# Attention into two mixture stages on one core: row maxima from a bf16 view of the f32r keys, one maximum row in the scores, v's scale through PSUM

## The chip, the cores and the metric

One core of a Trainium2 chip. The metric is the device time of one execution in microseconds (us). Engines are named as in the profile: PE is TensorE (PEld its weight loads), DVE VectorE, ACT ScalarE, POOL GpSimd, SP the engine whose queue issues the DMAs.

## The reference, cut to what matters

```python
# q, k, v: (2, 8, 1152, 64)
q_pool = q.reshape(B, H, S // 2, 2, D).mean(axis=3)          # 576 queries a head
scores = scale * np.matmul(q_pool, k.transpose(0, 1, 3, 2))
scores = scores - np.max(scores, axis=-1, keepdims=True)
attn = np.exp(scores)
attn = attn / (np.sum(attn, axis=-1, keepdims=True) + 1e-09)
attn_out = np.matmul(attn, v)
# then on x = attn_out as (1152, 512):
p = domain_probs / (domain_probs.sum(-1, keepdims=True) + 1e-09)
out = sum(p[:, e:e+1] * (np.maximum(x @ w1[e], 0.0) @ w2[e]) for e in range(4))
# then (out @ m1) * (out @ m2) @ m3 @ m_out
```

The maximum is only a shift of the exponent: the same shift stands in the numerator and in the sum.

## The kernel before

The 16 heads go through as eight pairs. Of a pair i, head s (0 or 1) has nine blocks of 128 keys. `plan_scores` makes scores with keys on partitions: for each block, two bf16 matmuls of `K2`, `Q2` (low parts, and in the first rows the maximum and a constant against rows of -1) and two f32r matmuls of `K1`, `Q1`, into a PSUM tile `s`. ACT takes the exponential into `pf` (line 581), POOL makes its low part `pl` (line 592), and `plan_av` multiplies both by the two halves of v (`vt`, lines 614 and 616).

While pair i's scores and products run, pair i+1 is made ready, all on the same engines:

- `plan_k`: PE transposes the keys into PSUM (`kt`, line 278, first two thirds, then the last third). ACT copies them as f32r words (`KAB`, line 281) and once more as bf16 (`KB`, line 284). DVE takes the remainder `KL` (line 287).
- `plan_v`: DVE takes v's absolute row maxima (`vm`, line 493), PE spreads them over the partitions (`vp`, line 497), and `bounds` on DVE (lines 481, 484, 485) makes the scale `vs` in three steps: mask the exponent, multiply and bound, invert. The second step reads and writes SBUF.
- `plan_q`: PE transposes the pooled queries (`qt`, line 345), ACT copies them as f32r (`QH`, line 357), then twice as bf16 into `QZ` (lines 354, 358), where each head's queries stand on their own 64 rows and the other rows are zero. DVE takes the remainder `QL` (line 348). POOL copies a last piece (line 352).
- `plan_max`: PE multiplies `QZ` by `KB` into PSUM tiles `mp` (line 415, three matmuls of 384 columns a query block), DVE reduces each (line 418). When a head's blocks are done, PE transposes the maxima (`mr`, line 452), ACT rounds them to bf16 (`mh`, line 456), DVE takes what that left (`ml`, line 460), and SP writes the two as rows 0 and 1 of `Q2` with four DMAs (lines 465, 466). Row 2 holds a constant shift.
- `plan_spread`: SP copies `KAB`, `KL`, `QH`, `QL`, `QZ` to `K1`, `K2`, `Q1`, `Q2`.

The first pair has short ways of its own: `plan_k_now`, and `turn_now`, which transposes the maxima split into two bf16 parts (`MT`, lines 439 to 441).

The order on each engine is written out by hand. Every step is put into an agenda with a time (18 units a pair), the agenda is sorted, and each engine gets its instructions in that order. The constants at the head of the file (`VR`, `VE`, `TURNS`, `KT`, ...) are those times.

Two PSUM work tiles serve all the preparing: `w0` (two banks) and `w1` (one bank), one buffer each. In `w0` come `kt`'s first part, `qt` and the wide `mp` in turn; in `w1` `mr`, `kt`'s last part, `vp` and the narrow `mp`. So a PE instruction that writes one of them waits until the readers of the tile before are done, and what stands behind it on PE waits too.

After the attention come four experts (`up`, `dn`) and the second mixture (`wf`, `gt`, `o`), from 257 us of the span on.

Of the kernel before, what the change touches and what calls it, by code (L numbers as in the profile page):

```python
# [11 lines left out]
TURNS = (1.13, 1.53, 1.73, 3.03)  # L12
TURN0 = (0.05, 0.45, 0.55, 0.65)
KH = 0.39
# [9 lines left out]
KS = 0.1  # L24
KS0 = 0.01
# [11 lines left out]
VE = 1.85  # L37
# [82 lines left out]
def tile_kernel(ctx: ExitStack, tc: tile.TileContext, q, k, v, dp, w1, w2, mw1, mw2, mw3, mwo, out):  # L120
# [79 lines left out]
    MT = k_p.tile([P, 2, NB + 1], F32, name="MT")  # L200
# [6 lines left out]
    KAB, KL, KB, QH, QL = {}, {}, {}, {}, {}  # L207
# [52 lines left out]
    def plan_k(i, t):  # L260

        def start():
            KAB[i] = kq_p.tile([P, S], F32R, tag="kab", name=f"kab{i}")
            KB[i] = kq_p.tile([P, S], BF16, tag="kb", bufs=1, name=f"kb{i}")
            KL[i] = ha_p.tile([P, S], BF16, tag=f"ha{i % 2}", name=f"kl{i}")
# [3 lines left out]
        for g in range(2):  # L269
# [13 lines left out]
            def short(g=g, rows=rows):  # L283
                nc.scalar.copy(out=rows(KB[i]), in_=st[g][:, :, :PC])

# [7 lines left out]
            at(t + KT[g] + KH + KS, short)  # L293
            at(t + KT[g] + KH + KL_, lo)

    def plan_k_now(t):
# [3 lines left out]
        def pe(n):  # L300
            if n == 0:
                pft[0, 0] = ph_p.tile([P, NC, T], F32, tag="pf", name="pf0_0")
                KAB[0] = kq_p.tile([P, S], F32R, tag="kab", name="kab0")
                KB[0] = kq_p.tile([P, S], BF16, tag="kb", bufs=1, name="kb0")
# [5 lines left out]

        def short(n):
            dst = KB[0][:, n * PC : (n + 1) * PC]
            if n == 1:
                nc.vector.tensor_copy(dst, st[n])
            else:
                nc.scalar.copy(out=dst, in_=st[n])
# [14 lines left out]
        for n in range(3):  # L331
            at(t + 0.1 * n, pe, n)
            at(t + 0.1 * n + KS0, short, n)
# [3 lines left out]
    def plan_q(i, t, tv):  # L337
# [12 lines left out]
        def one(lo, hi, to):  # L350
            if lo:
                nc.gpsimd.tensor_copy(QZ[64:128, to : to + hi - lo], f32(QH[i][64:128, lo:hi]))
            else:
                nc.scalar.copy(out=QZ[64:128, to : to + hi - lo], in_=st[0][64:128, lo:hi])
# [3 lines left out]
        at(tv + 0.02, lambda: nc.scalar.copy(out=QZ[0:64, :T], in_=st[0][0:64, :T]))  # L358
# [34 lines left out]
    def plan_max(i, s, times):  # L393
# [11 lines left out]
        def pe(j, g):  # L405
# [6 lines left out]
            for n, third in enumerate(THIRDS[g]):  # L412
                sl = slice(third * PC, (third + 1) * PC)
                o = j * P + (T + TL if s else 0)
                mm(ps[:, n, :PC], QZ[:, o : o + P], KB[i][:, sl], start=True, stop=True)  # L415
# [13 lines left out]
        def end():  # L429
# [7 lines left out]
            if (i, s) == (0, 0):  # L437
                mb = tiny.tile([P, NB + 1], BF16, tag="mb", bufs=1, name="mb")
                nc.vector.tensor_copy(mb, mf)
                nc.vector.tensor_copy(MT[:, 0, :], mb)  # L440
                nc.vector.tensor_tensor(out=MT[:, 1, :], in0=mf, in1=MT[:, 0, :], op=ALU.subtract)

        def turn_now():

            ps = work(0, "mr0").rearrange("p n c -> p (n c)")
            for j in range(NB + 1):
                nc.tensor.transpose(ps[0:2, j * P : (j + 1) * P], MT[:, :, j], ident)
            nc.scalar.copy(out=Q2[s][0:2], in_=ps[0:2, :T])
# [5 lines left out]
        def cut_hi():  # L454
            m = st["h"] = tiny.tile([NB + 1, P], BF16, tag="mh", bufs=1, name=f"mh{i}_{s}")
            nc.scalar.copy(out=m, in_=st["r"][: NB + 1, 0, :P])

        def cut_lo():
# [920 lines left out]
```

## Time and profile before

| what | value |
|---|---|
| median of 3 runs | 812.67 us (812.42 to 814.46) |
| span of the profiled execution | 809.9 us, of which the page gives no other time |
| busy PE, DVE, ACT, POOL | 779.1, 597.3, 404.1, 295.9 us |
| granted TensorE clock, mean | 0.999 |

The span runs from the first to the last instruction; the runs' times also hold what lies around it (812.67 against 809.9). A busy PE counts an instruction from its start to its modelled end, and matmuls overlap, so PE's share is no measure of how full it is; how far two matmuls start apart is.

### The profile page before, as it was taken

The numbers are of one execution on the slowest core, as the hardware profiler recorded it, in microseconds if no ns is written. First come the engines' busy times: TensorE is split into PE (matmuls) and PEld (weight loads), VectorE is DVE, ScalarE is ACT, GpSimd is POOL, SyncE is SP. The second block draws the span as 40 slices with busy tenths as digits, with TensorE's granted clock in tenths as the row PEclk, the third lists the DMA queues.
The fourth block names the chain that finished last, engine by engine and source line by source line (L and its number), as shares of the span: only waits on it lengthen the run. The fifth ranks groups of instructions, "written<-read, shape, count | busy, mean of one in ns | idle before, by whom it ended". The sixth has DMA issues, their size and how long they took to land.

```text
span 809.9 us, 15666 instructions
## 1 busy us (share of the span) xinstructions
PE 779.1 (96%) x6301; PEld 493.2 (61%) x6301; DVE 597.3 (74%) x1067; ACT 404.1 (50%) x738; POOL 295.9 (37%) x277
## 2 busy tenths in 40 slices
PE   7799999999999999999999999999999999999998
PEld 6477777777776555555555555555554446655787
DVE  6888888887966666779878999979878877872000
ACT  3665666566584443444434567545554545553111
POOL 5679877987760000001101125303331223442100
PEclk9999999999999999999999999999999999999999
DMA  7856765673610221223312333221476752200011
GB/s 173 210 134 144 170 142 121 161 176 74 153 54 2 70 90 51 79 79 105 104 63 94 104 105 101 82 78 53 121 140 121 175 128 71 93 1 1 18 49 52
DMA packets 87255, 79.70 MB, mean 98 GB/s; under 512 B 51024, under 2 KB 69712, under 8 KB 87184
## 3 DMA queue, kind: packets, MB, share of 16 engines
q1 hardware_dynamic: 87184, 78.72, 37.3%
q8 instruction: 49, 0.80, 0.4%
q14 instruction: 22, 0.18, 0.1%
HBM read 51.92 MB, written 2.36 MB: 67 GB/s over the span
## 4 chain that ended last, share of the span: by engine, by line
PE 74%; DVE 16%; DMA 4%; ACT 3%; issue 1%; SPq 1%; POOL 0%; ACTq 0%; DVEq 0%; POOLq 0%
PE dn L785 19%; PE up L745 18%; PE gt L1317 12%; PE o L1333 6%; PE wf L1286 5%; DVE mx L418 5%; PE av L616 4%; PE s L571 3%; PE mp L415 3%; DMA rw<-in_moe_w 2%; DVE vt L550 2%; PE av L614 2%; DMA rk<-in_k 1%; DVE w L716 1%; DMA Q<-qh 1%
## 5 line engine op out<-in xcount | busy, mean ns | idle before, releaser
L785 PE MATMUL dn<-w,h 128*128 128x512 f16 x840 | 184.2, 379 | 0.4 <-DVE h L756 0.4
L592 POOL TENSOR_TENSOR pl<-pf 128x576 f16<-128x576 f32 x141 | 163.9, 1190 | 16.2 <-ACT pf L581 15.6
L745 PEld LDWEIGHTS <-w 128*128 128x128 f16 x1152 | 111.5, 98 | 76.4 <-DVE w L716 1.0
L785 PEld LDWEIGHTS <-h 128*128 128x128 f16 x840 | 81.6, 98 | 97.2 <-issue 1.7
L581 ACT ACTIVATE pf<-s 128x576 f32<-128x576 f32 x144 | 91.6, 652 | 53.0 <-PE s L571 52.3
L745 PE MATMUL up<-xB,w 128*128 128x320 f16 x768 | 109.9, 299 | 0.5 <-DVE xB L834 0.5
L418 DVE TENSOR_REDUCE mx<-mp 128x1 f32<-128x768 f32 (+1 forms) x144 | 102.0, 751 | 10.6 <-PE mp L415 8.4
L884 POOL TENSOR_TENSOR wo<-wo,cv_a 128x512 f32<-128x512 f32 x20 | 25.8, 1293 | 224.9 <-DVE wo L881 126.9
L751 ACT ACTIVATE up<-up 128x320 f32<-128x320 f32 (+1 forms) x96 | 45.8, 477 | 114.7 <-PE up L745 105.0
L571 PE MATMUL s<-Q,K 128*128 128x288 bf16 (+1 forms) x576 | 97.0, 313 | 0.5 <-ACT pf L581 0.3
L745 PE MATMUL up<-xA,w 128*128 128x512 f16 x384 | 89.0, 379 | 0.3 <-DVE w L716 0.3
L616 PE MATMUL av<-vt,pf 128*128 128x65 f16 x720 | 83.7, 193 | 1.1 <-DVE XT L631 1.1
L616 PE MATMUL av<-vt,pl 128*128 128x65 f16 x720 | 84.4, 195 | 0.0
L756 DVE TENSOR_TENSOR h<-up,h 128x320 f16<-128x320 f32 (+1 forms) x94 | 50.1, 550 | 44.3 <-ACT h L752 43.9
L614 PE MATMUL av<-vt,pf 128*128 128x64 f16 x720 | 82.8, 193 | 0.0
L1317 PEld LDWEIGHTS <-mw 128*128 128x128 f16 x576 | 55.9, 98 | 36.9
L616 PEld LDWEIGHTS <-pf 128*128 128x128 bf16 x720 | 67.3, 99 | 9.0 <-DVE XT L631 2.1
L616 PEld LDWEIGHTS <-pl 128*128 128x128 f16 x720 | 66.9, 97 | 8.9 <-issue 3.9
L614 PEld LDWEIGHTS <-pf 128*128 128x128 bf16 x720 | 67.3, 98 | 4.8 <-issue 1.6
L415 PE MATMUL mp<-kb,QZ 128*128 128x384 bf16 x216 | 51.5, 325 | 14.3 <-DVE ql L348 6.2
L799 DVE SCALAR_TENSOR_TENSOR x2B<-dn,sh,x2B 128x512 f32<-128x512 f32 x75 | 52.9, 744 | 4.6 <-PE dn L785 3.9
L1317 PE MATMUL gt<-x2Bt,mw 128*128 128x320 f16 x384 | 53.5, 299 | 0.0
(189 smaller groups left out, 1182.0 us busy)
## 6 DMA issues: line engine op xcount, KB each, us to landing
rw<-in_moe_w SPq DMA_DIRECT2D x64, 512.0 KB
K<-kab SPq DMA_DIRECT2D x32, 288.0 KB
rk<-in_k SPq DMA_DIRECT2D x16, 288.0 KB
rv<-in_v SPq DMA_DIRECT2D x8, 576.0 KB
rq<-in_q SPq DMA_DIRECT2D x8, 512.0 KB
rw<-in_moe_w_out SPq DMA_DIRECT2D x8, 512.0 KB
Q<-qh SPq DMA_DIRECT2D x16, 144.0 KB
Q<-ql SPq DMA_DIRECT2D x16, 144.0 KB
```

The lines of the kernel that those rows point to most:

```text
L415: mm(ps[:, n, :PC], QZ[:, o : o + P], KB[i][:, sl], start=True, stop=True)
L418: nc.vector.tensor_reduce(out=mx[i, s][:, j, g : g + 1], in_=st.pop((j, g))[:, :, :PC], axis=AX.XY, op=ALU.max)
L571: mm(ps[:, n, :HALF], a[s][:, cs], b[s][:, n * HALF : (n + 1) * HALF], start=first, stop=not first,)
L581: nc.scalar.activation(out=two(pft[i, s][:, c, :]), in_=st["s"][:, :, :HALF], func=AF.Exp, scale=SCORE)
L592: nc.gpsimd.tensor_tensor(out=o, in0=f, in1=h, op=ALU.subtract)
L614: mm(t[:, j, 0:D], p, vt[s][:, c, 0:D], start=False, stop=False)
L616: mm(t[:, j, :], p, vt[s][:, c, D:], start=(c == 0 and n == 0), stop=(c == NC - 1 and n == 2))
L745: mm(p, w[:, a, c, fc * P : (fc + 1) * P], x[b][:, c, lo - o : hi - o], start=(c == 0 and a == b), stop=(c == KD - 1 and a == 1),)
L756: nc.vector.tensor_tensor(out=hl[:, fc, lo:hi], in0=st["p"], in1=hh[:, fc, lo:hi], op=ALU.subtract)
L785: mm(p, hid[n][a][:, fc, t * P : (t + 1) * P], w[:, b, fc, :], start=(fc == 0 and a == b), stop=(fc == 1 and a == 1),)
L799: nc.vector.scalar_tensor_tensor(out=acc, in0=st["p"], scalar=share, in1=acc, op0=ALU.mult, op1=ALU.add)
L1317: mm(p, mws[n][:, a, m * KD + c], x[:, b * KD + c, lo - o : hi - o], start=(c == 0 and a == b), stop=(c == KD - 1 and a == 1),)
```

## The change

Seven edits:

1. `KB` is gone. The matmuls for the maxima read the upper 16 bits of each f32r word of `KAB` as bf16, every second bf16 element of the row. The bf16 copies (ACT lines 284 and 316, DVE line 314) are gone.
2. `ml` and its two DMAs a head are gone: the maximum is one bf16 row of `Q2`, the constant is row 1.
3. `MT` and its three DVE steps are gone: the first pair's maxima are transposed as they are.
4. `mh` has two buffers where it had one.
5. In v's scale the masked exponents go to two columns of the PSUM tile `vp`, and the second step reads them there.
6. `vp` stands 0.95 units earlier in the agenda (`VE` 1.85 to 0.9).
7. ACT's two copies into `QZ` read `QH` in SBUF, where they read `qt` in PSUM.

```diff
--- before.py
+++ after.py
@@ -9,8 +9,8 @@
 from concourse.masks import make_identity
 
 TURN = 1.03
-TURNS = (1.13, 1.53, 1.73, 3.03)
-TURN0 = (0.05, 0.45, 0.55, 0.65)
+TURNS = (1.13, 1.53, 3.03)
+TURN0 = (0.05, 0.45, 0.65)
 KH = 0.39
 KL_ = 0.22
 QH_ = 1.05
@@ -21,8 +21,6 @@
 LO_DVE = ((), ())
 LASTD = ((3,), (1, 6))
 LOL = 2.45
-KS = 0.1
-KS0 = 0.01
 EX = 0.84
 EX2 = 0.85
 LO = 3.95
@@ -34,7 +32,7 @@
 VL = 1.96
 VL0 = -1.66
 VR = 4.22
-VE = 1.85
+VE = 0.9
 V1 = (5.5, 1.4)
 VL1 = 7.8
 QZ0 = 0.25
@@ -197,14 +195,14 @@
 
 
     QZ = k_p.tile([P, 2 * T], BF16, name="QZ")
-    MT = k_p.tile([P, 2, NB + 1], F32, name="MT")
     QP = k_p.tile([P, NB + 1, 2, D], F32, name="QP")
 
     PAIRS = [(i // (H // 2), 2 * (i % (H // 2))) for i in range(NPAIR)]
 
 
     rq, rt, rk, rv = {}, {}, {}, {}
-    KAB, KL, KB, QH, QL = {}, {}, {}, {}, {}
+    KAB, KL, QH, QL = {}, {}, {}, {}
+    upper = lambda ap: ap.bitcast(BF16).rearrange("p (c w) -> p c w", w=2)[:, :, 1]
     pft, pht, plt = {}, {}, {}
 
     def load_k(i):
@@ -261,7 +259,6 @@
 
         def start():
             KAB[i] = kq_p.tile([P, S], F32R, tag="kab", name=f"kab{i}")
-            KB[i] = kq_p.tile([P, S], BF16, tag="kb", bufs=1, name=f"kb{i}")
             KL[i] = ha_p.tile([P, S], BF16, tag=f"ha{i % 2}", name=f"kl{i}")
 
         at(t + KT[0], start)
@@ -280,9 +277,6 @@
             def hi(g=g, rows=rows):
                 nc.scalar.copy(out=rows(KAB[i]), in_=st[g][:, :, :PC])
 
-            def short(g=g, rows=rows):
-                nc.scalar.copy(out=rows(KB[i]), in_=st[g][:, :, :PC])
-
             def lo(g=g, rows=rows):
                 nc.vector.tensor_tensor(
                     out=rows(KL[i]), in0=st[g][:, :, :PC], in1=f32(rows(KAB[i])), op=ALU.subtract
@@ -290,7 +284,6 @@
 
             at(t + KT[g] + NEAR, pe)
             at(t + KT[g] + KH, hi)
-            at(t + KT[g] + KH + KS, short)
             at(t + KT[g] + KH + KL_, lo)
 
     def plan_k_now(t):
@@ -301,19 +294,11 @@
             if n == 0:
                 pft[0, 0] = ph_p.tile([P, NC, T], F32, tag="pf", name="pf0_0")
                 KAB[0] = kq_p.tile([P, S], F32R, tag="kab", name="kab0")
-                KB[0] = kq_p.tile([P, S], BF16, tag="kb", bufs=1, name="kb0")
                 KL[0] = ha_p.tile([P, S], BF16, tag="ha0", name="kl0")
             ps = work(1, "kt0_2") if n == 2 else ps_s.tile([P, 2, 512], F32, tag="s", name=f"kt0_{n}")
             st[n] = ps[:, 0, :PC]
             for m in range(3):
                 nc.tensor.transpose(st[n][:, m * P : (m + 1) * P], rk[0][:, 3 * n + m], ident)
-
-        def short(n):
-            dst = KB[0][:, n * PC : (n + 1) * PC]
-            if n == 1:
-                nc.vector.tensor_copy(dst, st[n])
-            else:
-                nc.scalar.copy(out=dst, in_=st[n])
 
         def hi(n):
             dst = KAB[0][:, n * PC : (n + 1) * PC]
@@ -330,7 +315,6 @@
 
         for n in range(3):
             at(t + 0.1 * n, pe, n)
-            at(t + 0.1 * n + KS0, short, n)
             at(t + 0.1 * n + 0.05, hi, n)
             at(t + 0.6 - 0.1 * n, lo, n)
 
@@ -351,11 +335,11 @@
             if lo:
                 nc.gpsimd.tensor_copy(QZ[64:128, to : to + hi - lo], f32(QH[i][64:128, lo:hi]))
             else:
-                nc.scalar.copy(out=QZ[64:128, to : to + hi - lo], in_=st[0][64:128, lo:hi])
+                nc.scalar.copy(out=QZ[64:128, to : to + hi - lo], in_=f32(QH[i][64:128, lo:hi]))
 
         at(t, pe)
         at(tv, lambda: nc.scalar.copy(out=QH[i], in_=st[0][:, :T]))
-        at(tv + 0.02, lambda: nc.scalar.copy(out=QZ[0:64, :T], in_=st[0][0:64, :T]))
+        at(tv + 0.02, lambda: nc.scalar.copy(out=QZ[0:64, :T], in_=f32(QH[i][0:64])))
         at(tv + QL_, lo)
         tz = tv + (QZ0 if i == 1 else QZ1)
         at(tz, one, 0, NB * P, T + TL)
@@ -412,7 +396,7 @@
             for n, third in enumerate(THIRDS[g]):
                 sl = slice(third * PC, (third + 1) * PC)
                 o = j * P + (T + TL if s else 0)
-                mm(ps[:, n, :PC], QZ[:, o : o + P], KB[i][:, sl], start=True, stop=True)
+                mm(ps[:, n, :PC], QZ[:, o : o + P], upper(KAB[i])[:, sl], start=True, stop=True)
 
         def reduce(j, g):
             nc.vector.tensor_reduce(
@@ -434,36 +418,26 @@
                 nc.vector.reduce_max(mf[:, :NB], mx[i, 1][:, :NB], axis=AX.X)
                 nc.vector.reduce_max(mf[:, NB:], mx[i, 0][:, NB], axis=AX.X)
             st["f"] = mf
-            if (i, s) == (0, 0):
-                mb = tiny.tile([P, NB + 1], BF16, tag="mb", bufs=1, name="mb")
-                nc.vector.tensor_copy(mb, mf)
-                nc.vector.tensor_copy(MT[:, 0, :], mb)
-                nc.vector.tensor_tensor(out=MT[:, 1, :], in0=mf, in1=MT[:, 0, :], op=ALU.subtract)
 
         def turn_now():
 
             ps = work(0, "mr0").rearrange("p n c -> p (n c)")
             for j in range(NB + 1):
-                nc.tensor.transpose(ps[0:2, j * P : (j + 1) * P], MT[:, :, j], ident)
-            nc.scalar.copy(out=Q2[s][0:2], in_=ps[0:2, :T])
+                nc.tensor.transpose(ps[0:1, j * P : (j + 1) * P], st["f"][:, j : j + 1], ident)
+            nc.scalar.copy(out=Q2[s][0:1], in_=ps[0:1, :T])
 
         def turn():
             ps = st["r"] = work(1, f"mr{i}_{s}")
             nc.tensor.transpose(ps[: NB + 1, 0, :P], st["f"], ident)
 
-        def cut_hi():
-            m = st["h"] = tiny.tile([NB + 1, P], BF16, tag="mh", bufs=1, name=f"mh{i}_{s}")
+        def cut():
+            m = st["h"] = tiny.tile([NB + 1, P], BF16, tag="mh", name=f"mh{i}_{s}")
             nc.scalar.copy(out=m, in_=st["r"][: NB + 1, 0, :P])
 
-        def cut_lo():
-            m = st["l"] = tiny.tile([NB + 1, P], BF16, tag="ml", bufs=1, name=f"ml{i}_{s}")
-            nc.vector.tensor_tensor(out=m, in0=st["r"][: NB + 1, 0, :P], in1=st["h"], op=ALU.subtract)
-
         def place():
-            for n, m in enumerate((st["h"], st["l"])):
-                dst = Q2[s][n : n + 1]
-                nc.sync.dma_start(out=dst[:, : NB * P], in_=m[:NB])
-                nc.sync.dma_start(out=dst[:, NB * P :], in_=m[NB : NB + 1, r])
+            dst = Q2[s][0:1]
+            nc.sync.dma_start(out=dst[:, : NB * P], in_=st["h"][:NB])
+            nc.sync.dma_start(out=dst[:, NB * P :], in_=st["h"][NB : NB + 1, r])
 
         e = times[-1] + 1 + ME
         at(e, end)
@@ -471,17 +445,18 @@
             at(e + TURN, turn_now)
             at(e + TURN + 0.01, warm, WARM_T)
             return
-        for d, f in zip(TURNS if i else TURN0, (turn, cut_hi, cut_lo, place)):
+        for d, f in zip(TURNS if i else TURN0, (turn, cut, place)):
             at(e + d, f)
 
 
     vs = {}
 
-    def bounds(p, up, down, low, top=2.0**-14):
+    def bounds(p, up, down, low, top=2.0**-14, mid=None):
+        mid = up if mid is None else mid
         nc.vector.tensor_scalar(
-            out=up.bitcast(I32), in0=p.bitcast(I32), scalar1=0x7F800000, scalar2=None, op0=ALU.bitwise_and
+            out=mid.bitcast(I32), in0=p.bitcast(I32), scalar1=0x7F800000, scalar2=None, op0=ALU.bitwise_and
         )
-        nc.vector.tensor_scalar(out=up, in0=up, scalar1=top, scalar2=low, op0=ALU.mult, op1=ALU.max)
+        nc.vector.tensor_scalar(out=up, in0=mid, scalar1=top, scalar2=low, op0=ALU.mult, op1=ALU.max)
         nc.vector.reciprocal(out=down, in_=up)
 
     def plan_v(i, t, te):
@@ -498,7 +473,7 @@
 
         def keep():
             x = vs[i] = tiny.tile([P, 2], F32, tag="vs", bufs=3, name=f"vs{i}")
-            bounds(st["p"][:, 0, :2], x, x, 2.0**-100)
+            bounds(st["p"][:, 0, :2], x, x, 2.0**-100, mid=st["p"][:, 0, 2:4])
 
         at(t, rows)
         at(te, spread)
@@ -893,8 +868,8 @@
         for s in range(2):
             nc.gpsimd.memset(Q2[s][0:64], 0.0)
             nc.gpsimd.memset(K2[s][0:64], 0.0)
-            nc.gpsimd.memset(K2[s][0:3], -1.0)
-            nc.gpsimd.memset(Q2[s][0:3], -SHIFT)
+            nc.gpsimd.memset(K2[s][0:2], -1.0)
+            nc.gpsimd.memset(Q2[s][0:2], -SHIFT)
             nc.gpsimd.memset(vt[s][:, :, 128:129], 1.0)
         nc.vector.memset(idle, 0.0)
         nc.vector.memset(QP[TL:P, NB], 0.0)
```

DVE, the place where pair 3 is made ready during pair 2 (`vt` is v's low part, `kl` the keys' remainder, `ql` the queries' remainder). Before, it reads:

```order
L550 SCALAR_TENSOR_TENSOR vt_119<-rv_752,vs_1073,vt_119 128x9x64
L460 TENSOR_TENSOR ml_1_1511<-mr_1_1490,mh_1_1504 5x128
L287 TENSOR_TENSOR kl_1494<-kt_0_1495,kab_1492 128x768
L493 TENSOR_REDUCE vm<-rv_1340 128x2
L287 TENSOR_TENSOR kl_1494<-kt_1_1528,kab_1492 128x384
L481 TENSOR_SCALAR vs_1641<-vp_1633 128x2
L484 TENSOR_SCALAR vs_1641<-vs_1641 128x2
L485 RECIPROCAL vs_1641<-vs_1641 128x2
L348 TENSOR_TENSOR ql_1582<-qt_1583,qh_1581 128x576
```

Now the same stretch reads:

```order
L525 SCALAR_TENSOR_TENSOR vt_119<-rv_736,vs_1008,vt_119 128x9x64
L281 TENSOR_TENSOR kl_1462<-kt_0_1463,kab_1461 128x768
L468 TENSOR_REDUCE vm<-rv_1311 128x2
L281 TENSOR_TENSOR kl_1462<-kt_1_1493,kab_1461 128x384
L456 TENSOR_SCALAR vp_1560<-vp_1560 128x2
L459 TENSOR_SCALAR vs_1566<-vp_1560 128x2
L460 RECIPROCAL vs_1566<-vs_1566 128x2
L332 TENSOR_TENSOR ql_1544<-qt_1545,qh_1543 128x576
```

`ml` is gone, and the middle step of the scale reads `vp`. The scale stood ahead of `ql` already; only for pair 1 it stands behind it, before and now.

ACT, the same place (`pf` are the exponentials of pair 2's scores). Before, it reads:

```order
L456 CAST mh_1_1504<-mr_1_1490 5x128
L281 CAST kab_1492<-kt_0_1495 128x768
L284 CAST kb_1493<-kt_0_1495 128x768
L581 ACTIVATE pf_0_1425<-s_0_3_1483 128x576
L281 CAST kab_1492<-kt_1_1528 128x384
L284 CAST kb_1493<-kt_1_1528 128x384
L581 ACTIVATE pf_0_1425<-s_0_4_1532 128x576
L581 ACTIVATE pf_0_1425<-s_0_5_1570 128x576
L357 CAST qh_1581<-qt_1583 128x576
L354 CAST QZ<-qt_1583 64x512
L358 CAST QZ<-qt_1583 64x576
```

Now the same stretch reads:

```order
L435 CAST mh_1_1472<-mr_1_1459 5x128
L278 CAST kab_1461<-kt_0_1463 128x768
L556 ACTIVATE pf_0_1394<-s_0_3_1452 128x576
L278 CAST kab_1461<-kt_1_1493 128x384
L556 ACTIVATE pf_0_1394<-s_0_4_1497 128x576
L556 ACTIVATE pf_0_1394<-s_0_5_1534 128x576
L341 CAST qh_1543<-qt_1545 128x576
L338 CAST QZ<-qh_1543 64x512
L342 CAST QZ<-qh_1543 64x576
```

Two copies are gone, and `QZ` comes from `qh`.

PE, the same place, around `vp` (`av` are the products with v). Before, it reads:

```order
L616 MATMUL av_1_1459<-vt_120,pl_1_1160 128x65
L497 LDWEIGHTS ones
L497 MATMUL vp_1633<-vm,ones 128x2
L616 LDWEIGHTS pf_1_1159
L616 MATMUL av_1_1459<-vt_120,pf_1_1159 128x65
L571 LDWEIGHTS K_0_123
```

Now the same stretch reads:

```order
L591 LDWEIGHTS pl_1_1133
L591 MATMUL av_1_1428<-vt_120,pl_1_1133 128x65
L472 LDWEIGHTS ones
L472 MATMUL vp_1560<-vm,ones 128x2
L591 LDWEIGHTS pf_1_1132
L591 MATMUL av_1_1428<-vt_120,pf_1_1132 128x65
```

`vp` stood just ahead of a block of scores, 33 products with v behind `qt`; now 9 of them stand between `qt` and `vp`, and the 24 others stand behind it. Nothing else moves on PE.

## Rows read from the trace of the kernel before

**Rows 1.** Windows: start:end, length, busy us of PE, PEld, DVE, ACT, POOL, clock, DMA.

```profile
79.00:106.00 27.00, 25.14 (x387) 20.53 (x386) 22.85 (x39) 16.90 (x30) 23.02 (x22) 1.00 0.63 148
```

**Rows 2.** Waits, 24 to 215 us: who waited for whom, total us, times, longest.

```profile
PE mp L415 <- DVE ql L348: 6.2, 6, 1.3
...
PE mp L415 <- DVE mx L418: 5.1, 9, 1.0
...
PEld kt L278 <- DVE ml L460: 3.9, 7, 1.5
```

**Rows 3.** Timeline of PE, 81 to 90 us: start, duration, [idle before <-releaser].

```profile
86.56 0.17 PE L497 MATMUL vp<-vm,ones 128*128 128x2 bf16 x1
...
87.38 0.67 PE L571 MATMUL s<-Q,K 128*128 128x288 bf16 x4
89.01 0.65 PE L415 MATMUL mp<-kb,QZ 128*128 128x384 bf16 x3 [0.96 <-DVE ql L348]
```

**Rows 4.** Chain of waits, 79 to 107 us: start, time on the chain, what.

```profile
101.14 0.51 PE s L571 x4
...
101.72 0.49 PE mp L415 x3
102.21 0.06 PE av L616 x2
```

**Rows 5.** Timeline of DVE, 78 to 107 us.

```profile
82.22 0.27 DVE L460 TENSOR_TENSOR ml<-mr,mh 5x128 bf16<-5x128 f32 x1
83.41 0.96 DVE L287 TENSOR_TENSOR kl<-kt,kab 128x768 bf16<-128x768 f32 x1 [0.92 <-ACT kb L284]
...
85.55 0.55 DVE L287 TENSOR_TENSOR kl<-kt,kab 128x384 bf16<-128x384 f32 x1
...
86.99 1.00 DVE L484 TENSOR_SCALAR vs<-vs 128x2 f32<-128x2 f32 x1
...
88.11 0.75 DVE L348 TENSOR_TENSOR ql<-qt,qh 128x576 fp32r<-128x576 f32 x1
```

**Rows 6.** Timeline of POOL, 85.9 to 87.9 us.

```profile
86.82 1.15 POOL L592 TENSOR_TENSOR pl<-pf 128x576 f16<-128x576 f32 x1
```

**Rows 7.** Instructions that touch `vs`: duration ns min/median/max, first and last start.

```profile
L546 ACT ACTIVATE vt<-rv,vs x16: 771/781/785, 20.7 to 229.2; 128x576 f16<-128x576 f32 x16
L550 DVE SCALAR_TENSOR_TENSOR vt<-rv,vs,vt x16: 808/1684/2918, 35.2 to 232.4; 128x576 f16<-128x576 f32 x16
...
L481 DVE TENSOR_SCALAR vs<-vp x8: 149/159/160, 19.2 to 195.6; 128x2 int32<-128x2 int32 x8
L484 DVE TENSOR_SCALAR vs<-vs x8: 169/1014/1042, 19.4 to 195.8; 128x2 f32<-128x2 f32 x8
```

**Rows 8.** Timeline of ACT, 78 to 107 us.

```profile
81.88 0.80 ACT L281 CAST kab<-kt 128x768 fp32r<-128x768 f32 x1 [0.40 <-PE kt L278]
...
85.75 0.64 ACT L357 CAST qh<-qt 128x576 fp32r<-128x576 f32 x1
...
87.02 0.63 ACT L358 CAST QZ<-qt 64x576 bf16<-64x576 f32 x1
```

**Rows 9.** Waits, 0 to 34 us.

```profile
PEld kt L278 <- DVE ml L460: 0.9, 1, 0.9
```

**Rows 10.** Chain of waits, 0 to 36 us.

```profile
8.48 0.48 ACT kb L316
...
28.07 0.70 ACT kb L284
...
31.87 0.77 DVE ql L348
```

**Rows 11.** Timeline of PE, 0 to 36 us: the first pair's maxima.

```profile
17.87 0.70 PE L447 MATMUL mr<-ident,MT 128*2 128x128 f32 x5 [0.72 <-DVE MT L441]
```

**Rows 12.** Timeline of SP's queue, 78 to 107 us: the last DMA of `ml`.

```profile
103.50 0.52 SPq L466 DMA_DIRECT2D Q<-ml  x1
```

**Rows 13.** Timeline of PE, 104.9 to 105.5 us.

```profile
105.00 0.77 PE L571 MATMUL s<-Q,K 128*128 128x288 bf16 x4
```

## The prediction

> **What bounds the kernel now.** I read the windows first. In the 27 us in which one pair runs and the next is made ready, PE shows 25.14 us busy, DVE 22.85, POOL 23.02, ACT 16.90, at clock 1.00 [rows 1]. Busy PE is near the span, but its matmuls overlap, so the place to look is where PE starts nothing. After the attention the page's slices show PE at 9 tenths almost to the end, and the change touches nothing there: a gain in the attention shifts the rest, and that is all.
>
> The waits give the places [rows 2]. Once in six of the seven preparations PE stands before the maxima's first matmul (`mp`) until DVE has made `ql`; before the last transposes of the keys (`kt`) until DVE has made `ml`, 3.9 us in seven; and before a later `mp` until DVE has reduced, 5.1 us in nine. PE's timeline shows the first of these: four score matmuls start at 87.38, take 0.51 [rows 3, 4], and the next matmul starts at 89.01, so PE loses 1.12 us (the trace's own 0.96 counts from a modelled end).
>
> DVE's timeline shows why `ql` is late: the middle step of v's scale, two numbers a partition, takes 1.00 us from 86.99 to 87.99 [rows 5]. POOL's instruction beside it runs from 86.82 to 87.97 [rows 6]: the step ends 0.02 us behind it. Of eight such steps the median is 1.014 and the shortest 0.169; the step ahead of it, which reads PSUM and does as much, never takes over 0.160 [rows 7]. So the step waits for POOL's instruction, and an operand in PSUM is what sets the two apart.
>
> **The change part by part.** All times are on the clock of the profiled execution (span 809.9); the runs' median 812.67 lies 2.8 above it, and I take the same saving from the median.
>
> *The place of the wait for `ql`.* The first key copy ends at 82.68 [rows 8]; with `kb` gone `kl` starts then and not at 83.41 [rows 5], 0.73 sooner. Its second part ends at 86.10 - 0.73 = 85.37. PE reaches `vp` sooner too: 24 products with v stand behind it now, at 0.03 each [rows 4] 0.72, and the `kt` wait ahead is gone, about 0.3. That is 86.56 - 1.02 = 85.54 [rows 3], so `vp` goes without a wait, by 0.17. The scale's steps start 0.43 behind `vp`, less the first step that is 0.2 earlier still; at 0.16 each for the two that touch PSUM and as much for the third they end near 86.3. `qh` ends at 86.39 - 0.3 = 86.1 [rows 8], and `ql` runs from 86.3 to 87.05. The second `QZ` copy, which ended at 87.65 [rows 8], ends 0.3 sooner but reads SBUF: between nothing and 0.14 more each (ACT's 576 columns out of SBUF take 0.781 [rows 7], out of PSUM 0.63 to 0.64 [rows 8]); I take 0.1 each, as the copy does not scale, and get 87.55. PE arrives at 87.89 - 0.3 = 87.6. So `ql` is no longer the last, `QZ` and PE come out level, and I leave 0.1 as a wait: 6 x (1.12 - 0.1) = **6.1 us**.
>
> *The wait for `ml`.* The tile that `kt`'s last part needs comes free with ACT's `mh` and no more with DVE's `ml`, which stands behind the long `vt` step. Of 3.9 us [rows 2] the first preparation's 0.9 [rows 9] belongs to the next term, 3.0 is left. In the second preparation `vt` is at its longest, 2.918 [rows 7]; there PE, freed, meets `vp` before `kl` is done, and I give 0.5 back: **2.5 us**.
>
> *The first preparation.* `kb` (0.70) and `ql` (0.77) both lie on the chain [rows 10]. `kb` is gone, and `ql` runs beside the `QZ` copies, which no longer share its PSUM tile. 1.47, less 0.1 for SBUF: **1.4 us**.
>
> *The start.* PE waits 0.72 us for `MT` [rows 11]; transposing the maxima as they are ends that. A key copy of 0.48 leaves the chain at 8.48 [rows 10], as `kab` takes its place. The reductions behind it are paced by DVE, so not all of it arrives: between 0.7 and 1.2 in all, **1.0 us**.
>
> *The DMAs.* Thirty issues of some 0.5 us [rows 12] leave SP's queue. The last of `ml` is issued until 104.02, and the first scores that need it start at 105.00 and take 0.77 instead of 0.67 [rows 3, 12, 13]: 0.1 in each of seven, **0.7 us**. Two DMAs fewer also bring forward the loads behind them; those are early already.
>
> *The maxima out of `KAB`.* The trace has no matmul that streams every second 16-bit element. Its nearest rows: four score matmuls of 288 columns, two bf16 and two f32r, take 0.51, three `mp` of 384 dense bf16 take 0.49 [rows 4]. Both are 1152 columns: 4 bytes a column stream at the speed of 2. Nothing faster is possible at a column's pace; the other end is half the pace. I take no change, since the f32r row reads the very same words.
>
> The Trainium skill gives, in SBUF — State Buffer, A bandwidth-pool intuition that's wrong, the moving operand's path as 2 bytes a lane and cycle at 2.4 GHz. By that figure a bf16 row spread over twice the bytes could run at half pace, and f32r would too; the trace's f32r does not, and the measurement decides.
>
> *At nothing.* The second buffer of `mh`, the shorter fills of POOL at the start (POOL idles behind them), and `mid` in PSUM beyond what is counted. POOL has 23.0 us of work in a pair [rows 1] that would shrink from 27 to some 25.6, so it stays covered.
>
> The sum: 6.1 + 2.5 + 1.4 + 1.0 + 0.7 = 11.7 us, **801.0 us**.
>
> **The rivals.**
>
> *The wait moves to `vp` (805).* PE stands behind `vp` earlier than before: its margin to `kl` goes from 86.56 - 86.10 = 0.46 to 0.17. `vt` on DVE waits for POOL's instructions as the scale did, from 0.808 to 2.918 [rows 7]; one more instruction of POOL, 1.15 [rows 6], less the 0.4 that `kl` waits for the key copy anyway and the 0.17, is 0.6 of PE's time. Six times that is 3.6: 804.6. For it: POOL is less ahead when PE is faster. Against: the median `vt`, 1.684 [rows 7], already waits for most of one.
>
> The Trainium skill says in SBUF — State Buffer, SBUF: two separate sides, that DVE and POOL share a pair of ports as an exclusive lock: whichever starts first holds it for its whole instruction. By that `vt` could lose one instruction of POOL, 0.808 + 1.15 = 1.96 at most; the trace's 2.918 is longer, so this rival is not capped there.
>
> *The later wait goes too (797).* PE's 5.1 us for DVE's reductions [rows 2] come behind a `vt` of 1.684 [rows 7]. Where POOL's phase falls better `vt` takes 0.81. Then up to 0.9 in each of some five preparations follows: 4 us more. Against: DVE and PE start that stretch together, and nothing in it is changed.
>
> *Slower: the 16-bit view streams at half pace (832).* Place: each `mp` matmul, 27 in a preparation; price 0.163 each [rows 4], 4.4 us a preparation, seven of them 31 us on PE, which is full there. Less the 11.7: 19 slower, 832. It decides from about 0.06 us a matmul on. Against it stands f32r's pace.
>
> *No gain (812).* DVE, not PE, could pace a pair, so that PE's freed time comes back as a wait for reductions. For: the 5.1. Against: DVE has 22.85 of 27 us [rows 1], and loses 0.8 of `vs` and two `ml` of 0.27 [rows 5].
>
> **How the numbers follow.** My forecast has 0.62, the wait at `vp` 0.15, the better phase 0.10, half pace 0.08, no gain 0.05. A measurement of this kernel tells some 0.3%, 2.4 us, from no change. The first three are faster: 0.87; no gain is 0.05, half pace 0.08. The range takes in the first three: below, 801.0 less 4 for the phase and 1.5 for the ends of the terms, 795.5; above, 804.6 with the terms at their poor ends, 807.5.
>
> **What would show it.** In the profile after: the scale's second step at 0.16 to 0.20 us in all preparations; `ql` done before the second `QZ`; `kt`'s wait for `ml` gone; at `mp` under 0.2 us of wait for `ql` or `QZ`; `mp` matmuls still 0.16 apart; a pair's period some 1.4 us shorter. It is wrong if `mp` matmuls start over 0.2 apart, if PE stands at `vp` for more than 0.3 us in most preparations, or if the wait for reductions grows by as much as the others shrink.

## The result and the profile after

| | median us | range |
|---|---|---|
| before | 813.50 | 812.42 to 814.46 (4 runs) |
| after | 802.80 | 801.50 to 805.03 (4 runs) |

The ratio is 0.987, 95% interval [0.9843, 0.9897]: 10.7 us less, where 11.7 were forecast. The profiled execution of after took 802.42 us with a span of 800.6; its span is 9.3 shorter than that of before. Each run's time lies 1.8 above its span, and not 2.8, so the profiled execution of before, with a span of 809.9, is one of some 811.7, below the median. Of the 9.3, 8.34 are there when the last `vt` starts (232.39 before, 224.05 after); the rest lies in the experts, where the change touches nothing.

The waits of after, from 24 to 215 us:

```profile
PE vp L472 <- DVE kl L281: 3.0, 5, 0.7
...
PE mp L399 <- DVE mx L402: 2.7, 5, 0.9
...
PE qt L329 <- DVE kl L281: 1.7, 2, 1.3
```

Two waits of [rows 2] are gone altogether, that for `ql` (6.2) and that for `ml` (3.9). The wait for reductions fell from 5.1 to 2.7. In their place PE waits longer at `vp`, 3.0 where it was 0.4, and at `qt`, 1.7 where it was 0.9.

DVE's timeline of after, in the preparation that [rows 5] shows of before:

```profile
78.67 1.78 DVE L525 SCALAR_TENSOR_TENSOR vt<-rv,vs,vt 128x576 f16<-128x576 f32 x1
80.79 0.96 DVE L281 TENSOR_TENSOR kl<-kt,kab 128x768 bf16<-128x768 f32 x1 [0.34 <-ACT kab L278]
...
83.93 0.16 DVE L459 TENSOR_SCALAR vs<-vp 128x2 f32<-128x2 f32 x1
...
84.21 0.76 DVE L332 TENSOR_TENSOR ql<-qt,qh 128x576 fp32r<-128x576 f32 x1
```

The scale's middle step takes 0.16 where it took 1.00, and `ql` ends at 84.97. It runs beside ACT's two `QZ` copies, 84.09 to 85.41, which read `QH` now. PE's timeline of the same place has the first `mp` right behind the scores, 0.51 after them, with no wait, where 1.63 lay between them [rows 3]:

```profile
85.09 0.67 PE L546 MATMUL s<-Q,K 128*128 128x288 bf16 x4
85.60 0.69 PE L399 MATMUL mp<-kab,QZ 128*128 128x384 bf16 x3
```

The instructions that touch `vs` in after (min/median/max ns), to be read beside [rows 7]:

```profile
L525 DVE SCALAR_TENSOR_TENSOR vt<-rv,vs,vt x16: 807/1496/4533, 32.4 to 224.1; 128x576 f16<-128x576 f32 x16
...
L459 DVE TENSOR_SCALAR vs<-vp x8: 159/159/160, 18.6 to 188.1; 128x2 f32<-128x2 f32 x8
```

All eight scale steps are short now. But the longest `vt` grew from 2.918 to 4.533. That one stands in the second preparation, and it costs. The two windows run from one pair's first `kt` to the next pair's, the second preparation and the third:

```profile
49.64:79.11 29.47, 26.89 (x390) 21.74 (x388) 24.27 (x37) 16.42 (x27) 24.26 (x25) 0.94 0.62 143
79.11:104.74 25.63, 25.01 (x389) 20.55 (x387) 21.66 (x37) 16.21 (x27) 22.83 (x23) 1.00 0.67 157
```

The third takes 25.63 us, where 27.16 were taken before (first `kt` at 81.03 and 108.19): 1.53 less. The second takes 29.47, where it took 28.39: 1.08 more. The timelines of DVE and PE say why:

```profile
49.21 4.53 DVE L525 SCALAR_TENSOR_TENSOR vt<-rv,vs,vt 128x576 f16<-128x576 f32 x1
```

```profile
54.66 0.77 PE L329 MATMUL qt<-ident,QP 128*128 128x128 f32 x5 [1.31 <-DVE kl L281]
56.38 0.16 PE L472 MATMUL vp<-vm,ones 128*128 128x2 bf16 x1 [0.71 <-DVE kl L281]
```

`kl` stands behind `vt` on DVE, and PE stands for `kl` first at `qt` and then at `vp`. Behind this the granted clock falls, as windows of that stretch show:

```profile
54.00:57.00 3.00, 1.63 (x34) 1.52 (x35) 2.68 (x6) 1.48 (x3) 0.69 (x2) 1.00 0.88 251
57.00:60.20 3.20, 3.20 (x29) 2.51 (x26) 0.82 (x2) 1.40 (x3) 3.20 (x4) 0.50 0.57 126
```

In the second window PE ran at 0.50, which is 1.2 GHz, and it did so until 60.40, for 3.4 us in all. By the starts of PE's instructions it had lost 1.48 and 0.87 us just before. If full clock had halved those 3.4 us, an estimate, all three make 4.05, and this preparation is 29.47 - 25.63 = 3.84 longer than the next. The clock does not fall in every execution: one of the four runs of after has a mean granted clock of 1.000, the three others 0.998.

### The profile page after: what moved, and what is told of

Its sections match the earlier page's. It is cut to its first block, busy times and chain, and to the rows that moved or that the text cites. A ratio compares the mean times of both kernels' runs of the same rounds, so it can differ in the third digit from the quotient of the medians.

```text
span 800.6 us, 15559 instructions
## 1 busy us (share of the span) xinstructions
PE 779.1 (97%) x6301; PEld 493.9 (62%) x6301; DVE 590.5 (74%) x1048; ACT 398.1 (50%) x722; POOL 294.5 (37%) x277
## 4 chain that ended last, share of the span: by engine, by line
PE 84%; DVE 9%; DMA 2%; SPq 2%; POOL 1%; ACT 1%; issue 1%; POOLq 0%; ACTq 0%
PE dn L760 22%; PE up L720 22%; PE gt L1292 12%; PE o L1308 6%; PE s L546 5%; PE wf L1261 5%; PE av L591 4%; PE mp L399 3%; DVE vt L525 2%; DVE mx L402 2%; PE av L589 2%; POOL pl L567 1%; DVE kl L281 1%; DMA rw<-in_moe_w 1%; DMA rk<-in_k 1%; DVE vm L468 1%
## 5 line engine op out<-in xcount | busy, mean ns | idle before, releaser
L591 PEld LDWEIGHTS <-pf 128*128 128x128 bf16 x720 | 67.4, 99 | 10.7 <-DVE XT L606 2.0
L399 PE MATMUL mp<-kab,QZ 128*128 128x384 bf16 x216 | 52.8, 335 | 4.3 <-DVE mx L402 3.8
```

Source lines behind the costliest of these rows:

```text
L399: mm(ps[:, n, :PC], QZ[:, o : o + P], upper(KAB[i])[:, sl], start=True, stop=True)
L591: mm(t[:, j, :], p, vt[s][:, c, D:], start=(c == 0 and n == 0), stop=(c == NC - 1 and n == 2))
```

## The experiments

The theory at the start, **A**, is the forecast's: each term stands by itself, and the scale's wait is the largest. The rivals (**B** to **G**) are told in the expectations. What to look for in each is where PE stands. To compare them I take the stretch of before from 108.19 to 135.33 (first `kt` of pair 4 to that of pair 5) in every kernel but the two with both `vt` steps moved, and count at each place how much later PE starts than it usually does behind the same instruction:

| kernel | `kt` | `vp` | first `mp` | later `mp` | sum | period | less the sum |
|---|---|---|---|---|---|---|---|
| before | 0.39 | | 1.12 | 0.86 | 2.37 | 27.14 | 24.77 |
| scale through PSUM alone | 1.70 | | 0.69 | 0.19 | 2.58 | 27.35 | 24.77 |
| one row alone | | | 0.85 | 0.18 | 1.03 | 25.90 | 24.87 |
| both of these | | | 0.83 | 0.18 | 1.01 | 25.91 | 24.90 |
| after, two rows back | 1.68 | | | 0.81 | 2.49 | 27.39 | 24.90 |
| after | | 0.84 | | | 0.84 | 25.70 | 24.86 |
| after, scale in SBUF | | 0.84 | 0.27 | 0.80 | 1.91 | 26.81 | 24.90 |
| after, `vp` late | | | 0.24 | 0.46 | 0.70 | 25.65 | 24.95 |
| after, bf16 key copy back | | 0.84 | | 0.25 | 1.09 | 25.91 | 24.82 |
| after, `vt` of head 0 moved | | | | 0.77 | 0.77 | 25.62 | 24.85 |
| the same, `vp` late | | | 0.27 | 0.53 | 0.80 | 25.63 | 24.83 |

The last column hardly moves: in this stretch, what the edits do to the time is what they do to PE's waits.

**Scale through PSUM alone.** The kernel before with edit 5 and nothing else.

```diff
-            bounds(st["p"][:, 0, :2], x, x, 2.0**-100)
+            bounds(st["p"][:, 0, :2], x, x, 2.0**-100, mid=st["p"][:, 0, 2:4])
```

> The kernel before with edit 5 alone: the masked exponents of v's scale stay in PSUM. Theory A (the scale's second step waited for POOL and held ql, and ql held PE): the step falls from 1.0 to 0.16 us in every preparation, ql ends 0.85 us sooner, PE's next limit is its own arrival at 87.9 or the QZ copy at 87.65, so some 0.85 us in six preparations: about 5 us faster than before, 0.994. Theory B (the relief of ACT by the dropped key copies is what counted, the step was hidden): PE waits for a QZ copy or the next reduction instead, under 1 us faster, 0.999 to 1.0.

Measured: 813.05 us, ratio 1.0013 [1.0001, 1.0026]. No gain; the expectation missed. Its waits, 24 to 215 us:

```profile
PEld kt L278 <- DVE ml L460: 10.3, 7, 2.7
...
PE mp L415 <- DVE ql L348: 3.3, 6, 0.6
```

The wait for `ql` fell from 6.2 to 3.3, and that for `ml` rose from 3.9 to 10.3. DVE's, POOL's and PE's timelines show one of the seven:

```profile
109.15 3.03 DVE L551 SCALAR_TENSOR_TENSOR vt<-rv,vs,vt 128x576 f16<-128x576 f32 x1
112.11 0.27 DVE L460 TENSOR_TENSOR ml<-mr,mh 5x128 bf16<-5x128 f32 x1
```

```profile
106.00 5.56 POOL L593 TENSOR_TENSOR pl<-pf 128x576 f16<-128x576 f32 x5
```

```profile
112.43 0.55 PE L278 MATMUL kt<-ident,rk 128*128 128x128 f32 x3 [1.53 <-DVE ml L460]
```

`vt` now lasts until 0.6 after POOL's run of five ends at 111.56; `ml` stands behind it, and `kt` waits for `ml`. What PE gained at `mp` it lost at `kt`.

Nor was the scale all that held `ql`. ACT's and DVE's timelines of the same place show `ql` right behind ACT's second `QZ` copy, which reads `qt` in PSUM here; the scale was done at 117.24:

```profile
116.89 0.63 ACT L358 CAST QZ<-qt 64x576 bf16<-64x576 f32 x1
```

```profile
117.56 0.76 DVE L348 TENSOR_TENSOR ql<-qt,qh 128x576 fp32r<-128x576 f32 x1 [0.32 <-ACT QZ L358]
```

**After without edit 5.** The line above, undone in the kernel after.

> The changed kernel with edit 5 undone. In the changed kernel the second step now runs just when POOL starts: in four of seven preparations beside a POOL instruction, in the others while POOL is idle; and ql has some 0.5 us to spare before the maxima's matmul. Theory A, with that: about 0.3 us lost in three or four preparations, about 1 us slower than the changed kernel (0.988 to 0.989 of before). Theory A in its plain form, the step's price as before: 5 to 6 us slower (0.994). Theory B: as the changed kernel, 0.987.

Measured: 803.37 us, 0.9888 [0.9871, 0.9904]. Against after's 0.987 the intervals overlap; by the middle values the edit is worth 0.0018 of 813, 1.5 us, and not 6. Of the eight scale steps three still wait, at 0.93, 0.93 and 1.11 us; the five others take 0.17, as they no longer meet a POOL instruction. So the 1.5 hides larger shifts: the stretch of the table, where one of the three stands, is 1.11 longer than in after, the first preparation is 0.73 longer, and the second is 1.20 shorter, 28.27. In the second PE stands for the same 1.48 and 0.87 us as in after, but the granted clock stays at 1.00.

**After with `vp` at its old place** (edit 6 undone).

```diff
-VE = 0.9
+VE = 1.85
```

> The changed kernel with edit 6 undone: vp back behind 24 more products with v. Theory A: PE's 3.0 us of waiting at vp for the keys' remainder go; the scale and ql come 0.7 us later in each preparation, of which 0.5 are to spare: between 1.5 us faster and 1.5 us slower than the changed kernel. Rival C (the early vp is needed, since without it ql holds PE again): 0.4 us and more in six preparations, 2.5 us or more slower (0.990).

Measured: 801.07 us, 0.9853 [0.9833, 0.9873]. The early `vp` brings nothing; late it is no worse, and of the waits at `vp` only the first preparation's 0.4 is left, while `vt` still takes up to 4.5. In the stretch of the table the period is 25.65, with 0.70 of waits at `mp`.

**After with the bf16 key copy back** (edit 1 undone; `mp` reads a dense row again).

```diff
-                mm(ps[:, n, :PC], QZ[:, o : o + P], upper(KAB[i])[:, sl], start=True, stop=True)
+                mm(ps[:, n, :PC], QZ[:, o : o + P], KB[i][:, sl], start=True, stop=True)
...
+            at(t + KT[g] + KH + 0.1, short)
```

> The changed kernel with edit 1 undone: the bf16 key copies are back on ACT (DVE for one of the first pair), and the maxima's matmuls stream dense bf16. Theory A: the keys' remainder comes 0.7 us later, PE stands that much longer at vp in five preparations, the first preparation loses 0.7, and matmuls keep their pace: 4 to 5 us slower than the changed kernel (0.992). Theory B: nearly all of the gain is lost, 9 us or more slower (0.998). If the strided view cost PE something, this run would start those matmuls closer together than the changed kernel does, by over 0.01 us.

Measured: 803.87 us, 0.9895 [0.9878, 0.9912]: by the middle values 2 us, half of what theory A expected. PE waits at `vp` in all seven preparations here, 4.2 us. The median from start to start of `mp` is 0.163, against 0.171 in after, so the spread row is what slows `mp`, by 0.008, a little under the 0.01 that the expectation named. The copies' place in the table's stretch is small too: a period of 25.91 against 25.70.

**One row alone.** The kernel before with edits 2 to 4 (`ml`, its DMAs and `MT` gone, two buffers of `mh`).

```diff
-        for d, f in zip(TURNS if i else TURN0, (turn, cut_hi, cut_lo, place)):
+        for d, f in zip(TURNS if i else TURN0, (turn, cut, place)):
```

> The kernel before with edits 2 to 4 alone: one maximum row, no ml, no split of the first pair's maxima; key copies, scale and QZ as before. Theory D (the first run of experiments: DVE's vt step waits for POOL, 0.8 to 4.5 us, whatever else is mended, and costs PE only where something that PE needs soon stands behind it; ml did, for kt): the kt waits for ml go (0.4 in five preparations, 1.6 in one), the start gains 0.7, the DMAs 0.7: 4 to 5 us faster than before (0.994 to 0.995), with the wait of mp for ql left at about 1.1. Theory E (the edits only help together, each freed wait comes back elsewhere): within 1 us of before, as the scale alone.

Measured: 805.84 us, 0.9915 [0.9894, 0.9936]: 6.9 us by the ratio, more than expected. Waits of PE, 24 to 215 us:

```profile
PE mp L414 <- DVE ql L347: 4.8, 6, 0.9
...
PE mp L414 <- DVE mx L417: 3.3, 6, 0.9
```

No `kt` waits for `ml`. `ql`'s wait is mostly there, though the scale's middle step waits for POOL in one preparation only (0.93; in the six others it takes 0.17): in five of these six `ql` starts 0.03 us behind ACT's second `QZ` copy. The surplus is in the table's column of the later `mp`: 0.86 became 0.18, as head 1's `vt` ahead of those reductions takes 1.03 there and not 1.70.

**After with two rows back** (edits 2 to 4 undone, the others kept).

```diff
-        for d, f in zip(TURNS if i else TURN0, (turn, cut, place)):
+        for d, f in zip(TURNS if i else TURN0, (turn, cut_hi, cut_lo, place)):
```

> The changed kernel with edits 2 to 4 undone: two rows of maxima, ml and its DMAs, the first pair's split. Theory D: vt keeps its 3 us in some preparations and ml behind it holds kt, 1.7 us in each of four to five, and the start loses 0.7: 7 to 9 us slower than the changed kernel (0.996 to 0.998 of before). Theory E: as the other edits undone one by one, 1 to 2 us slower (0.989).

Measured: 812.06 us, 0.9995 [0.9979, 1.0011]. Without edits 2 to 4 nothing is left of the gain, slightly less than theory D expected; the four other edits together are worth nothing alone. Its waits:

```profile
PEld kt L276 <- DVE ml L445: 11.8, 7, 3.0
```

`mp` waits for neither `ql` nor `QZ` here, and PE stands at `kt` instead, 1.68 in the stretch of the table.

**Both `vt` steps moved, in after and in before.** If DVE's `vt` is what hurts, it can stand where POOL is idle. For pairs 1 to 6 the low part of head 0 went from 1.96 to 5.0 units of the agenda into the pair, that of head 1 to 5.7, counted from the pair's middle.

```diff
+VLS = (5.0, 5.7)
...
-                at(t + 9 * s + (VL if i + s else VL1) + (VLZ if i == NPAIR - 1 and not s else 0), v_lo, i, s)
+                at(t + 9 * s + (VLS[s] if 0 < i < NPAIR - 1 else VL if i + s else VL1) + (VLZ if i == NPAIR - 1 and not s else 0), v_lo, i, s)
```

> The changed kernel with both vt steps of pairs 1 to 6 moved: head 0's from behind the maxima to behind the keys' remainder, where POOL waits for qh, head 1's from ahead of a reduction that PE waits for to a place where DVE idles. Theory D: head 0's vt falls to 0.8 to 1.3 us, PE's waits at vp (3.0 us) and the second pair's stretch at half clock go, the wait of mp for a reduction (2.7) shrinks: 4 to 6 us faster than the changed kernel (0.981). Theory E, or a vt that is no limit: within 1 us of it (0.987).

> The kernel before with the same two vt steps moved and nothing else changed. Theory D: ml no longer stands behind vt, so kt's waits go (3 us in six preparations); the scale's step and ql stay, so the wait for ql takes most of the 0.4 in five of them back; the wait for a reduction, 5.1 us, shrinks by some 4: 5 to 6 us faster than before (0.993). If vt is no limit: within 1 us of before.

Measured: 831.62 us, 1.0231 [1.0206, 1.0255] in after; 834.09 us, 1.0270 [1.0244, 1.0297] in before. Both are far slower, the opposite of what was expected. In before, head 1's step takes 5.38 to 5.66. DVE's and POOL's timelines of the kernel after with both moved:

```profile
70.05 7.00 DVE L526 SCALAR_TENSOR_TENSOR vt<-rv,vs,vt 128x576 f16<-128x576 f32 x1
...
89.13 0.81 DVE L526 SCALAR_TENSOR_TENSOR vt<-rv,vs,vt 128x576 f16<-128x576 f32 x1
```

```profile
69.50 0.73 POOL L247 TENSOR_TENSOR QP<-rq 128x256 f32<-128x256 f32 x1
70.20 3.35 POOL L568 TENSOR_TENSOR pl<-pf 128x576 f16<-128x576 f32 x3
73.51 0.72 POOL L247 TENSOR_TENSOR QP<-rq 128x256 f32<-128x256 f32 x1
74.19 2.25 POOL L568 TENSOR_TENSOR pl<-pf 128x576 f16<-128x576 f32 x2
83.18 3.36 POOL L568 TENSOR_TENSOR pl<-pf 128x576 f16<-128x576 f32 x3 [6.74 <-ACT pf L557]
```

Head 0's step takes 0.81, as meant. Head 1's landed in a POOL run without a gap and takes 7.00: it ends 0.6 after the last of six POOL instructions that started behind it, none of them held up. The reductions stand behind it on DVE, and PE behind them:

```profile
PE mp L400 <- DVE mx L403: 27.0, 7, 5.3
```

The granted clock fell too: it was 0.50 from 75.60 to 82.30, and 0.979 over the whole span. So the miss is the place of head 1's step, and it is the strongest showing of the wait that this study is about.

The run on the kernel before shows one thing more. `ml` is kept there, and with head 0's `vt` no longer ahead of it `kt` waits for it in the first preparation alone, which was not changed:

```profile
PEld kt L279 <- DVE ml L461: 0.9, 1, 0.9
```

In before it waited in seven, 3.9 us [rows 2]. (The other `ml` of a pair stands behind head 1's step there, and `mp` waits for it, 22.0 us.)

**Only head 0's `vt` moved** in after, then the same with `vp` late.

```diff
-VLS = (5.0, 5.7)
+VLS = (5.0, 1.96)
```

> The changed kernel with only head 0's low-part step of v (vt on DVE) moved from 1.96 to 5.0 units into the pair, for pairs 1 to 6; head 1's stays where it is. Theory F (vt is what still costs: its wait for POOL makes PE stand 3.0 us at vp, 1.7 us at qt and brings the stretch at half clock in the second preparation): vt of head 0 at 0.81 in all six, waits at vp and qt near 0, no stretch at 0.50, and 3 to 4.5 us less than the changed kernel: ratio to the kernel before 0.981 to 0.984. Theory G (the waits at vp are made good elsewhere, as DVE and POOL set the pace there): 0.986 to 0.989, the period of a pair still 25.6. If head 1's vt shows over 4 us again although it was not moved, the long wait does not come from its own place.

> As the run with head 0's vt moved alone, and vp back at its old place (VE 1.85). F: with vt out of the way kl is early, vp waits at either place for nothing, so the same time within 0.2 per cent. If the early vp is what brings the wait at vp, 0.5 to 1 us less than the run with vt moved alone only if that one still shows such waits.

Measured: 798.93 us, 0.9831 [0.9807, 0.9855]; with `vp` late 799.37, 0.9836 [0.9813, 0.9858]. By medians 3.9 us below after, by the ratios 3.2 (0.987; the intervals just overlap, the ranges of the runs do not: 798.19 to 801.02 against 801.50 to 805.03). The fastest kernel of the study, level with the same with `vp` late. Its `vt`, and the stretch that ran at half clock in after:

```profile
L526 DVE SCALAR_TENSOR_TENSOR vt<-rv,vs,vt x16: 807/972/1692, 32.5 to 219.8; 128x576 f16<-128x576 f32 x16
```

```profile
57.00:60.20 3.20, 3.20 (x49) 2.48 (x47) 2.53 (x4) 1.72 (x4) 3.20 (x3) 1.00 0.84 181
```

The time is F's, but half of the reason is G's. The second preparation takes 25.67 us and not 29.47, with the stands at `qt` and `vp` and the half clock gone; the sixth takes 25.83 and not 26.95; the first is 0.70 longer. There the gain lies. In the third to the fifth it is within 0.1: where PE waited at `vp` that wait is gone and another has come at the later `mp`, so that the period stays at 25.6, as PE's timeline shows in the stretch of the table:

```profile
116.40 0.50 PE L400 MATMUL mp<-kab,QZ 128*128 128x384 bf16 x2 [0.61 <-DVE mx L403]
```

**One row and the scale through PSUM**, on the kernel before: edits 2 to 5, the two diffs shown above together.

> The kernel before with the single maximum row (edits 2 to 4) and v's scale through PSUM (edit 5), nothing else. Theory E (the scale's wait only counts once ml no longer stands behind vt): the two together gain more than the one row alone (0.9915) by most of the wait at mp that is left there, about 1.0 us in four to six preparations, less what kb's 0.7 then holds: 2 to 3 us, ratio 0.988 to 0.989. Rival (the scale through PSUM never pays, as vt grows by as much): 0.991 to 0.993, the same as the one row alone.

Measured: 804.41 us, 0.9895 [0.9872, 0.9918], against 0.9915 [0.9894, 0.9936] for the one row alone. Between E's and the rival's numbers, and not told apart by intervals that overlap. The waits tell why it is little: as with the one row alone, `ql` stands behind ACT's copies out of `qt`'s PSUM tile, and PE still waits for it. With the one row alone the scale step waited for POOL in one preparation, so edit 5 had little left to mend.

```profile
PE mp L414 <- DVE ql L347: 4.2, 6, 0.9
```

## Why the prediction was right, and where not

The sum came out (801.0 forecast, 802.80 measured, 10.7 of the 11.7 us), but in part by luck: the two largest terms were wrong, one too large and one too small. Of the six signs that it named three are there throughout: the scale step at 0.16 in all, no wait for `ml`, none at `mp` for `ql` or `QZ`. Three are there in part: `ql` is done ahead of the second `QZ` in three preparations of seven (84.97 and 85.41 in the third), and 0.2 to 0.4 behind it in four; the period is shorter by 1.4 to 1.6 in the third to fifth preparations, by 2.17 in the first and 0.25 in the sixth, and longer by 1.08 in the second; and the pace of `mp` is nearly kept (below). Of the signs against it one came: PE stands over 0.3 us at `vp` in five preparations of seven (in the first of these it did before).

*The place of the wait for `ql`, 6.1 us: the wait went, the credit was wrong.* Two steps failed. One is the reading that the scale's middle step is why `ql` is late: with that step at 0.16, PE's loss at the first `mp` in the pair of the table only falls from 1.12 to 0.69, as `ql` then stands behind ACT's copies out of `qt`. Edit 7, which the forecast named for this only in the first preparation, takes `ql` out from behind them. No run has edit 7 alone or leaves it out alone; from edits 2 to 5 (0.9895) to all seven (0.987) edits 1, 6 and 7 bring 2.0 us together, with intervals that overlap. The other step is the one that priced this wait by itself and took `vt` for fixed. Edit 5 alone gains nothing, and all edits but 2 to 4 together gain nothing. A shorter wait at `mp` changes where DVE's `vt` meets POOL's run; in the pair of the table `vt` grew from 1.7 to 3.03, and as long as `ml` stands behind it, `kt` gives the time back.

*The wait for `ml`, 2.5 us: mis-sized.* By itself it is worth 6.9, with the other edits around it 0.9995 - 0.987 = 0.0125 of 813, 10.2 us. What edit 2 takes away is not 3.9 us of waits but the link by which a longer `vt` reached PE at `kt`. The experiment undoes edits 3 and 4 with it; edit 3 touches only the start, and that the second buffer of `mh` is worth nothing was argued, not tried.

*The first preparation, 1.4, and the start, 1.0: the one low, the other right.* From the first `kt` to the first `mp` it was 7.07 us (26.22 to 33.29) and is 5.14 (25.39 to 30.53), 1.9 less. With the key copy back it is 5.98, with two rows back 5.47, so some 0.3 of the 1.9 belong to `ml`. The first pair's maxima are turned without a wait at 16.92, where it was 17.87 [rows 11], 0.95 sooner:

```profile
16.92 0.71 PE L426 MATMUL mr<-ident,mf 128*1 128x128 f32 x5
```

*The DMAs, 0.7: open.* The last maxima are issued until 99.31 and the first scores that need them take 0.68 at 101.63, where it was 0.77 [rows 13]; that is 0.09 as assumed, and no run isolates it.

*The maxima out of `KAB`, taken at no change: nearly.* Three `mp` take 0.53 on after's chain of waits, 0.49 before [rows 4]:

```profile
85.25 0.51 PE s L546 x4
85.76 0.53 PE mp L399 x3
```

That is 0.013 each, and 27 in each of seven preparations make some 2.5 us at most; the median from start to start, 0.171 against 0.162, gives 1.7 (0.163 with the dense row back in after). So a bf16 row spread over f32r words streams at 95% of the dense pace. By the figure that the prediction took from the Trainium skill (SBUF — State Buffer, A bandwidth-pool intuition that's wrong) it could have run at half pace; the trace goes against that, and the rival of 832 is out.

*The rivals.* Two of them happened at once. "The wait moves to `vp`" was priced at 0.6 a preparation, and the table has 0.84. "The later wait goes too" was priced at up to 0.9, and the table has 0.86 less. In that stretch they cancel. In the sixth period, with both waits there, 26.95 us, the gain is only 0.25.

*Left out altogether: the second preparation.* I gave 0.5 back there by a `vt` of 2.918. It became 4.533, PE stood twice, and the clock fell: 1.08 lost where a gain was forecast. Without the fall of the clock the loss is gone, but no gain comes, as far as one execution shows: with the scale in SBUF the same preparation, with the same stands, took 28.27 at full clock, and 28.39 before.

**What stays open.** Why PE's waits add up to 0.70 to 0.84 in this stretch in after, with `vp` late and with head 0's `vt` moved, whichever place they stand at, with the period at 25.6 to 25.7, was not settled; with the scale in SBUF they add up to 1.91. Nor was head 0's `vt` moved in the kernel before with all else kept, which would price `vt` ahead of `ml` alone.

## What to carry to other kernels

A wait is not worth what the profile shows beside it as long as a step of variable length upstream can take the time back: ask what else stands behind that step on its engine, and who waits for it. Here the two-number scale looked like the culprit, and mending it alone gained nothing; the long `vt` ahead of a five-row `ml` mattered more. Taking the dependant away gained most, and moving head 0's step into a gap of the other engine gained some 3 us more. Ask also what else the late step stands behind: `ql` stood behind ACT's copies as well as behind the scale. Before moving such a step, look at the other engine's timeline at the new place for an idle stretch that is longer than the step.

## What the runs showed that was not expected

**A DVE step can wait for POOL's whole run, not for one instruction.** `vt` has its operands in SBUF and takes 0.81 alone. In the kernel before and in all eleven experiments as well as in after, every `vt` over 2.6 us ends about 0.6 after the end of a run of POOL, at which POOL fell idle; none lies between 1.8 and 2.6, and those of 1.8 or less got in ahead of the next POOL instruction, or met none. So there are two kinds, the long and the short. POOL's timeline in after shows the short kind, beside the `vt` of 78.67: two `pl` in a row take 2.25 together (the first row), and 2.77 where `vt` got in between (the second row, which shares an instruction with the first).

```profile
77.58 2.25 POOL L567 TENSOR_TENSOR pl<-pf 128x576 f16<-128x576 f32 x2 [0.91 <-ACT pf L556]
```

```profile
78.69 2.77 POOL L567 TENSOR_TENSOR pl<-pf 128x576 f16<-128x576 f32 x2
```

And here is the long kind, beside the `vt` of 49.21, which ends at 53.74; five `pl` run on at 1.11 each until 53.12:

```profile
47.55 5.57 POOL L567 TENSOR_TENSOR pl<-pf 128x576 f16<-128x576 f32 x5
```

The Trainium skill says in SBUF — State Buffer, SBUF: two separate sides, of a DVE step with two SBUF inputs and a POOL instruction that reads SBUF, that whichever starts first has the shared ports for its whole instruction and the other blocks. `vt` and `pl` are such a pair. One instruction lost agrees with that; four and seven in a row do not follow from it. Which of the two happens was not settled: steps that were issued at nearly the same point of a POOL instruction, 104.31 and 117.72 in after, took 3.05 and 0.84.

**Half clock after two short stands, but not always.** The granted clock was 0.50 from 57.00 to 60.40 in after, behind a stretch in which PE was busy 1.63 of 3.00 us, and 1.00 in the same stretch with `vt` moved. With the scale in SBUF, and with the key copy back, PE stood for as long at the same two places (1.48 to 1.51 and 0.87 to 0.88 us), and the clock stayed at 1.00. What tells these executions apart was not settled.
